# Attention and a mixture of experts: one scale per batch in place of a scale per token for the attention output, the second batch's values read twice, every step issued in a new order

## The chip, the cores and the metric

One Trainium2 chip, one of its cores. The time is device microseconds of one execution of the whole kernel; the number that counts is the median of three runs. The engines work side by side, each through its own queue in order: PE (TensorE, matmuls, with PEld for the loading of its stationary operand), DVE (VectorE), ACT (ScalarE), POOL (GpSimd) and SP (here only the issue of DMAs).

## The reference

Two parts, one behind the other: attention in which each query keeps only its 32 highest scores, and a dense mixture of four experts on its output.

```python
B, H, S, D = 2, 8, 576, 64
scores = (1 / np.sqrt(D)) * np.matmul(q, k.transpose(0, 1, 3, 2))
kth = np.partition(scores, -32, axis=-1)[..., -32:-31]
scores = np.where(scores >= kth, scores, -1e9)
attn = np.exp(scores - np.max(scores, axis=-1, keepdims=True))
attn = attn / (np.sum(attn, axis=-1, keepdims=True) + 1e-9)
x = np.matmul(attn, v).transpose(0, 2, 1, 3).reshape(B * S, H * D)   # 1152 x 512
p = domain_probs / (domain_probs.sum(-1, keepdims=True) + 1e-9)      # 1152 x 4
out = sum(p[:, e:e + 1] * (np.maximum(x @ w1[e], 0) @ w2[e]) for e in range(4))
```

## The kernel before

**Tiles and units.** The 1152 tokens are ten tiles: four of 128 rows and one of 64 in each batch. The 64-row tile of batch 0 comes first. A unit is one head of one tile (for a 64-row tile two heads side by side, 64 partitions each), so there are 72 units: 0 to 3 are the first tile, 4 to 11 the second, and so on; batch 1 begins at unit 36.

**A unit** goes through: scores on PE into PSUM (`emit_qk`, tile `ps`, two buffers); four MAX8 and three MATCH_REPLACE8 on DVE (`topk_op`), which find the 32 highest; an exponential on ACT (`emit_exp`); the mask (`emit_mask`), for units 0 to 19 one DVE instruction that reads `ps` (line 697, "DVE w"), later mostly on ACT and POOL; a split of the weights into two float16 halves (`emit_a`); a DMA transposition on SP's queue (`emit_at`, tile `at`); and the product with the values (`emit_av`). The mask is the last reader of `ps`, so the scores of unit u wait for the mask of unit u-2.

**Split operands.** All large matmuls run in float16 with each operand as a high and a low half: x = hi + lo. `split` makes these: mode "a" scales the raw values in place on ACT, copies to float16 on ACT and subtracts on POOL (a "lo"); mode "d" copies with the scale on ACT and makes the lo with one DVE instruction. The scale is a power of two from the mean square (`pow2`: two or three small DVE instructions). Weights (32 quarter matrices, tiles `w`), keys (`khl`, `kt`), values (`vt`), queries (`qhl`) and the attention output (`xhl`) are all split so. For keys and values of batch 0 there is one scale for all heads (`prep_first`), for batch 1 one for each head (`prep_kv`, squares on ACT, a matmul with ones, `pow2`); the inverse of the value scales stands in `sv`, and `emit_x_half` multiplies by it.

**Attention output.** `emit_x_half` divides by the sum of the weights; `emit_x_end` then squares x on ACT (`x_square`, line 805), in a 64-row tile adds the two halves' squares with matmuls against `pmat` (`x_cross`, line 809), takes one scale per token (`x_total`, `pow2`), scales in place and copies on ACT (`x_hi`, lines 820 and 822), makes the lo on POOL or DVE, puts inverse scale times probability into `pf` (`x_lo`, line 834) and issues the transposition to `xt`.

**Experts.** `moe` runs 8 half steps of `m1` (x against `w1`, lines 906 to 908), `h_hi`/`h_lo` (relu and split), `m2` (lines 949) for each tile; `evac` multiplies by the column of `pf`, adds up over the experts and writes the tile out.

**Order.** Nothing is scheduled at run time. Each step is an event with a place, and the table `ISSUE`, written into the kernel, has for each event and each of its pieces the position in the order of issue. `MASKS`, `NB`, `X_LO`, `EVAC`, `KV1`, `V0`, `K0`, `W_MODE` say per step which engine does it. Raw queries, keys and values of batch 1 pass through the pool `raw`, which has two buffers; a load into it waits until the reader of the buffer's former content is done.

Of the kernel before, what the change touches and what calls it, by code (L numbers as in the profile page):

```python
# [40 lines left out]
    kb_k=-64, kb_v=-5, kb_load=2, kb_sq=14, kb_tot=18, kb_scale=24, kb_fin=29,  # L41
)
MANUAL = ('PE', 'DVE', 'Activation', 'Pool', 'SP')
H_LO = ('ddpd', 'pppppppp', 'pppppddp', 'pdpppppd', 'pppppppp', 'pppppppp', 'pppppppp', 'pppppppp', 'pppppppp', 'pppp')

MASKS = 'ddddddddddddddddddddrrrrrrrrrdrrrrrrrrrddrdrdrrrrrrrrrrrrrrrrrrrrrrrrrrr'
NB = 'aaaaddddddddddddddadpdddddddpdapppapapdadppappppppaaapaapappaaaaapaappap'

X_LO = "dpdppppppp"
Q_LO = 'pppppppppp'  # L50

W_MODE = 'aaaaaaadaaaaaaaaaaaaaaaaaaadaaaa'
# [1162 lines left out]
```

## Time and profile before

| what | value |
|---|---|
| median of three runs | 567.65 us (565.24 to 568.88) |
| the profiled execution | 569.06 us, its span 567.3 us |
| mean granted TensorE clock | 0.951 |
| PE busy | 514.7 us, 91% of the span |
| DVE busy | 450.2 us, 79% |
| ACT busy | 384.2 us, 68% |
| POOL busy | 367.6 us, 65% |

The profiled execution has 1.8 us around its span and lies 1.4 us above the median. Busy shares are means over stages that differ: what the time turns on is which engine has no idle time in which stage, so the rows further down are cut by stage.

### The profile page before, as it was taken

The page shows a single profiled execution, that of the slowest core. Times are in us where ns is not written, and L with a number is a line of the kernel's source. Part 1 is how long each engine was busy: PE and PEld are TensorE (multiplying, and loading weights), DVE is VectorE, ACT ScalarE, POOL GpSimd, SP SyncE. Part 2 cuts the span into 40 slices and gives each one's busy share as a digit, 9 for nine tenths or more (in the row PEclk, how much of TensorE's full clock was granted, in tenths as well). Part 3 has the DMA queues.
Part 4 walks back from the last instruction along what each step waited for, and adds up shares of the span by engine and source line. Part 5 has one row for each costly group of instructions (what it writes and reads, how often), then busy time and mean ns, then how long its engine had stood idle before and what let it go on. Part 6 is the DMA issues. An engine that isn't in the chain of part 4 may idle for free.

```text
span 567.3 us, 16339 instructions
## 1 busy us (share of the span) xinstructions
PE 514.7 (91%) x6680; PEld 387.4 (68%) x6680; DVE 450.2 (79%) x1008; ACT 384.2 (68%) x668; POOL 367.6 (65%) x414
## 2 busy tenths in 40 slices
PE   4878667585999999999999999999999999999996
PEld 3556555373876668777876877777677777667864
DVE  2898999999899999999999998999988984700101
ACT  2678989989466696887876987767867746342311
POOL 0065988997665875887676878768865783451311
PEclk9988578876999999999999999999999999999999
DMA  9687878952263344555655644353443232231000
GB/s 222 205 223 184 260 239 182 239 91 51 60 93 64 62 97 90 82 86 107 131 103 127 95 96 83 64 101 62 57 78 72 43 64 41 41 41 44 12 2 29
DMA packets 140460, 57.05 MB, mean 101 GB/s; under 512 B 128864, under 2 KB 132064, under 8 KB 140384
## 3 DMA queue, kind: packets, MB, share of 16 engines
q1 hardware_dynamic: 136960, 53.12, 44.6%
q10 hardware_dynamic: 3424, 2.88, 1.7%
q8 instruction: 52, 0.85, 0.6%
q14 instruction: 24, 0.20, 0.1%
HBM read 24.14 MB, written 2.36 MB: 47 GB/s over the span
## 4 chain that ended last, share of the span: by engine, by line
PE 67%; DVE 17%; POOL 4%; DMA 4%; issue 3%; ACT 2%; SPq 1%; DVEq 0%; POOLq 0%; ACTq 0%
PE m L949 26%; PE m L906 10%; PE m L908 9%; PE m L907 9%; DVE m L646 6%; PE av L755 4%; PE ps L633 4%; DVE w L650 3%; DVE w L648 2%; DVE w L697 1%; DMA at<-a 1%; POOL h L931 1%; DMA xt<-xhl 1%; PE m L489 1%; DVE vt L426 1%
## 5 line engine op out<-in xcount | busy, mean ns | idle before, releaser
L949 PE MATMUL m<-w,h 128*128 128x512 f16 (+1 forms) x960 | 198.6, 384 | 0.9 <-POOL h L931 0.9
L908 PE MATMUL m<-xt,w 128*128 128x128 f16 (+1 forms) x1280 | 199.3, 215 | 0.0
L906 PE MATMUL m<-xt,w 128*128 128x128 f16 (+1 forms) x1120 | 179.0, 215 | 0.0
L907 PE MATMUL m<-xt,w 128*128 128x128 f16 (+1 forms) x1120 | 178.9, 215 | 0.0
L646 DVE MAX8 m<-w 128x8 f32<-128x576 f32 x216 | 161.5, 754 | 3.4
L949 PEld LDWEIGHTS <-h 128*128 128x128 f16 (+1 forms) x960 | 83.9, 102 | 90.9 <-issue 2.7
L931 POOL TENSOR_TENSOR h<-hf,h 128x512 f16<-128x512 f32 x65 | 75.3, 1158 | 85.9 <-ACT hf L924 79.3
L908 PEld LDWEIGHTS <-w 128*128 128x128 f16 x1280 | 123.8, 99 | 0.0
L906 PEld LDWEIGHTS <-w 128*128 128x128 f16 x1120 | 108.9, 99 | 3.1 <-issue 0.6
L907 PEld LDWEIGHTS <-w 128*128 128x128 f16 x1120 | 108.5, 99 | 2.4
L650 DVE MATCH_REPLACE8 w<-m,w 128x576 f32<-128x576 f32 x144 | 106.8, 742 | 0.0
L717 POOL TENSOR_TENSOR a<-w,a 128x512 f16<-128x512 f32 x68 | 78.9, 1163 | 15.1 <-ACT a L715 13.3
L690 ACT ACTIVATE w<-ps,nb,es 128x576 f32<-128x576 f32 x68 | 56.3, 829 | 42.0 <-DVE m L646 29.8
L917 ACT ACTIVATE h<-m 128x512 f16<-128x512 f32 x72 | 42.5, 592 | 60.2 <-PE m L908 43.3
L646 DVE MAX8 m<-ps 128x8 f32<-128x576 f32 x72 | 54.4, 755 | 31.5 <-PE ps L629 11.0
L707 POOL TENSOR_TENSOR w<-w,d 128x576 f32<-128x576 f32 x47 | 60.0, 1279 | 23.4 <-ACT d L704 21.7
L715 ACT ACTIVATE a<-w 128x576 f16<-128x576 f32 x68 | 45.8, 678 | 12.6 <-POOL w L707 8.6
L633 PE MATMUL ps<-kt,qa 128*128 128x288 f16 x128 | 36.7, 304 | 19.1 <-DVE w L697 19.0
L648 DVE MATCH_REPLACE8 w<-m,ps 128x576 f32<-128x576 f32 x72 | 53.8, 747 | 0.0
L976 DVE SCALAR_TENSOR_TENSOR o<-m,pf,o 128x512 f32<-128x512 f32 (+1 forms) x15 | 11.2, 745 | 50.6 <-PE m L949 42.4
L924 ACT ACTIVATE hf<-m 128x512 f32<-128x512 f32 x65 | 38.5, 592 | 5.5 <-POOL h L931 5.3
L755 PEld LDWEIGHTS <-at 128*128 128x128 f16 (+1 forms) x1008 | 37.1, 101 | 6.9 <-DMA at<-a 2.6
(172 smaller groups left out, 826.0 us busy)
## 6 DMA issues: line engine op xcount, KB each, us to landing
w<-in_moe_w_dram SPq DMA_DIRECT2D x16, 1024.0 KB, 8.1
qraw<-in_q_dram SPq DMA_DIRECT2D x8, 256.0 KB, 3.7
qb<-qa SPq DMA_DIRECT2D x16, 128.0 KB, 2.6
out_dram<-o ACTq DMA_DIRECT2D x8, 256.0 KB, 2.1
at<-a SPq DMA_TRANSPOSE x68, 3.3
vraw<-in_v_dram SPq DMA_DIRECT2D x2, 512.0 KB, 7.3
kraw<-in_k_dram SPq DMA_DIRECT2D x4, 256.0 KB, 3.4
vraw<-in_v_dram SPq DMA_DIRECT2D x4, 256.0 KB, 3.3
```

Of the source, the lines that this page charges most:

```text
L633: PE.matmul(ps[:, 0:288], lhsT=src[:, x, :], rhs=kt[x].rearrange("p c n -> p (c n)")[:, ks], start=(j == 0), stop=(j == 1))
L646: DVE.max(m, s_t[u] if r == 0 else w_t[u])
L648: DVE.match_replace(rows2(w_t[u]), m, s_t[u], NEG)
L650: DVE.match_replace(w_t[u], m, w_t[u], NEG)
L707: POOL.tensor_tensor(w, w, g, op=OP.mult)
L717: POOL.tensor_tensor(a[:, 640:1152], w[:, 0:512], a[:, 0:512], op=OP.subtract)
L755: PE.matmul(o, lhsT=att[:, blk, ps], rhs=r, start=(i == 0), stop=(i == len(seq) - 1))
L906: PE.matmul(o, lhsT=HI[e, 0, c][:, fc], rhs=xs(0, c), start=(c == 0), stop=False)
L907: PE.matmul(o, lhsT=HI[e, 0, c][:, fc], rhs=xs(1, c), start=False, stop=False)
L908: PE.matmul(o, lhsT=LO[e, 0, c][:, fc], rhs=xs(0, c), start=False, stop=(c == 3))
L931: POOL.tensor_tensor(h[:, 1], hf, h[:, 0], op=OP.subtract)
L949: PE.matmul(y[z * 64:z * 64 + M, :], lhsT=h_t[es, qd][:, p // 2, h0:h0 + M], rhs=w, start=(fc == 0 and p == 0), stop=(fc == 7 and p == 2))
```

## The change

**Attention output.** `x_square`, `x_cross`, `x_total`, the scaling in `x_hi` and `pf` are gone, with `pmat`. The scale of x is now one number per batch, taken from the values: the inverse of the value scale times a constant goes into `ix`, the division in `emit_x_half` brings it in with the constant `K_X`, and `evac` takes `pn` (batch 0, multiplied once by `ix` in `norm_x0`) or `pniw` (batch 1, multiplied once in `v1_scale`).

**Values of batch 1.** They need one scale for all eight heads ahead of the first split. So they are loaded twice: first as `nraw` in four loads of two heads, each squared as a whole on ACT (`v1_square`), then one matmul with ones, a sum and `pow2`; later again as `vraw`, two heads at a time, for the split itself. `prep_kv` becomes `prep_k1` and does the keys alone.

**Modes and order.** `V0` and `K0` become "a" throughout, of the later units four instead of five are masked on DVE and other ones, `NB`, `EVAC`, `KV1`, `X_LO`, `H_LO`, `W_MODE` change in places, and `ISSUE` is a new table.

```diff
-MASKS = 'ddddddddddddddddddddrrrrrrrrrdrrrrrrrrrddrdrdrrrrrrrrrrrrrrrrrrrrrrrrrrr'
...
+MASKS = 'ddddddddddddddddddddrrrrrrrrrrrrrrdrrrrrrrddrdrrrrrrrrrrrrrrrrrrrrrrrrrr'
...
-V0 = 'daddaaaa'
-K0 = 'daadaaaa'
+V0 = 'aaaaaaaa'
+K0 = 'aaaaaaaa'
...
-C_QK, C_V0, C_X, C_W1, C_W2 = 11, 14, 5, 10, 14
+C_QK, C_V0, C_W1, C_W2 = 11, 14, 6, 14
+K_X = 2.0 ** 5
...
+        def v1_square(p):
+            r = raw1["n", p]
+            r = r.rearrange("p h c d -> p (h c d)")
+            ACT.activation(r.bitcast(BF16)[:, 0:10 * D], r, AF.Square, accum_out=v1[:, p:p + 1])
+
+        def v1_total():
+            vs1["pt"] = bank(ps_m2, "m2")
+            PE.matmul(vs1["pt"][:, 0:4], lhsT=ones, rhs=v1, start=True, stop=True)
...
             if t == tiles[0]:
-                DVE.tensor_scalar(r2, total, EPS, None, op0=OP.add)
+                DVE.tensor_scalar(r2, total, EPS, ix[:, 0:1], op0=OP.add, op1=OP.mult)
             else:
-                vs = sv_r if rest else sv[:, t[0], half * 4:half * 4 + 4]
-                DVE.scalar_tensor_tensor(r2, total, EPS, vs, op0=OP.add, op1=OP.mult)
+                DVE.tensor_scalar(r2, total, EPS, K_X, op0=OP.add, op1=OP.mult)
...
             def x_hi():
-                x = st["x"]
-                if X_LO[g] == "p":
-                    ACT.activation(x, x, AF.Copy, scale=st["s"])
-                    yield
-                ACT.activation(st["hl"][:, 0:n], x, AF.Copy, scale=1.0 if X_LO[g] == "p" else st["s"])
...
+                ACT.activation(hl[:, 0:n], x_t[t][:, 0:n], AF.Copy)
...
-            at(steps[0], x_square)
-            if rest:
-                at(steps[0] + 0.1, x_cross)
-            at(steps[1], x_total)
             at(steps[2], x_hi)
...
         for p in range(4):
...
+            at(f1 + P["kb_n"] + 8 * p, load_raw, "n", p)
+            at(f1 + P["kb_n"] + 8 * p + 7, v1_square, p)
```

What the new order does, at three places. In the names, `ps` with a number is one unit's scores, `vt` with a number one head's values of batch 0, `w` with a number one weight matrix.

On DVE, at the first pass over the scores of unit 8, before:

```order
L646 MAX m<-ps_904 128x8
L286 TENSOR_SCALAR wpt<-m_858 128x1
L697 SCALAR_TENSOR_TENSOR w<-ps_769,m,w 128x576
L648 MATCH_REPLACE w<-m,ps_904 128x576
L686 TENSOR_SCALAR nb<-m,es 128x1
L646 MAX m<-w 128x8
L426 SCALAR_TENSOR_TENSOR vt_143<-vraw_153,vps,vt_143 128x5x64
L650 MATCH_REPLACE w<-m,w 128x576
```

and now:

```order
L655 MAX m<-ps_883 128x8
L659 MATCH_REPLACE w<-m,w 128x576
L657 MATCH_REPLACE w<-m,ps_883 128x576
L655 MAX m<-w 128x8 x2
L1060 TENSOR_SCALAR pn<-pn,ix 128x20
L420 SCALAR_TENSOR_TENSOR w_124<-w_124,ws,w_125 128x1024
L281 TENSOR_SCALAR wpt<-m_843 128x1
L706 SCALAR_TENSOR_TENSOR w<-ps_815,m,w 128x576
```

The lo of a head's values has left this queue, `norm_x0` has come into it, and a weight lo has come into these rows (before, the one DVE weight lo of this part of the program stood eleven rows ahead of them).

On POOL, around the lo parts of the third weight matrix, before:

```order
L424 TENSOR_TENSOR vt_145<-vraw_153,vt_145 128x5x64
L424 TENSOR_TENSOR khl_152<-kraw_151,khl_152 128x5x64
L719 TENSOR_TENSOR a<-w,a 128x64
L424 TENSOR_TENSOR w_125<-w_125,w_126 128x1024
L834 TENSOR_SCALAR pf<-pn,xpr 128x4
L424 TENSOR_TENSOR w_125<-w_125,w_126 128x1024
L424 TENSOR_TENSOR w_125<-w_125 128x1024 x2
```

and now (the third matrix is called w_124 here):

```order
L418 TENSOR_TENSOR w_124<-w_124,w_125 128x1024
L726 TENSOR_TENSOR a<-w,a 128x512
L728 TENSOR_TENSOR a<-w,a 128x64
L418 TENSOR_TENSOR vt_139<-vraw_152,vt_139 128x5x64
L418 TENSOR_TENSOR vt_146<-vraw_152,vt_146 128x5x64
L418 TENSOR_TENSOR vt_143<-vraw_152,vt_143 128x5x64
L813 TENSOR_TENSOR xhl<-x,xhl 128x256
L418 TENSOR_TENSOR vt_142<-vraw_152,vt_142 128x5x64
L418 TENSOR_TENSOR w_124<-w_124 128x1024
```

Four of the eight value lo parts and the first tile's x lo now stand between two weight lo parts; `pf` is gone.

On SP, about a third of the way through its queue, now:

```order
L816 DMA_TRANSPOSE xt<-xhl 128x8x128
L325 DMA nraw<-in_v_dram 128x2x256
L328 DMA nraw<-in_v_dram 64x2x64 x2
L734 DMA_TRANSPOSE at<-a 128x9x128 x3
L325 DMA nraw<-in_v_dram 128x2x256
L328 DMA nraw<-in_v_dram 64x2x64 x2
L734 DMA_TRANSPOSE at<-a 128x9x128 x2
L325 DMA nraw<-in_v_dram 128x2x256
```

where before there were transpositions and query loads alone:

```order
L837 DMA_TRANSPOSE xt<-xhl 128x8x128
L725 DMA_TRANSPOSE at<-a 128x9x128 x2
L406 DMA qb<-qa 64x1024
L408 DMA qb<-qa 64x1024
L725 DMA_TRANSPOSE at<-a 128x9x128 x2
L400 DMA_TRANSPOSE qa<-qhl 128x8x128
```

The four `nraw` loads, three DMAs each, stand ahead of `at` transpositions that PE's value products wait for.

## Rows read from the trace of the kernel before

**Rows 1.** Stretches of the span: busy us of each engine (instructions), clock, DMA.

```profile
0.00:31.86 31.86, 21.05 (x166) 14.12 (x167) 18.97 (x50) 16.82 (x37) 2.13 (x16) 1.00 0.77 198
31.86:81.01 49.15, 35.32 (x449) 29.74 (x449) 46.73 (x108) 40.96 (x62) 38.63 (x32) 0.69 0.81 225
81.01:134.60 53.59, 33.45 (x565) 27.37 (x562) 51.48 (x129) 49.24 (x62) 49.62 (x39) 0.83 0.76 173
134.60:450.00 315.40, 312.49 (x3915) 235.61 (x3915) 296.38 (x649) 233.84 (x433) 232.45 (x282) 0.99 0.45 84
450.00:562.40 112.40, 112.35 (x1593) 80.55 (x1591) 35.16 (x75) 43.30 (x77) 44.73 (x49) 1.00 0.17 34
```

**Rows 2.** Waits of PE over the whole span: us in total, times, longest.

```profile
PE ps L633 <- DVE w L697: 19.0, 9, 4.8
...
PE av L755 <- DMA at<-a: 1.9, 2, 1.4
...
PE m L906 <- DMA xt<-xhl: 1.5, 2, 1.0
```

**Rows 3.** Timeline of PE: scores of unit 17; 48 first-layer matmuls, first and last.

```profile
134.63 0.40 PE L633 MATMUL ps<-kt,qa 128*128 128x288 f16 x1 [4.80 <-DVE w L697]
...
140.79 0.23 PE L906 MATMUL m<-xt,wx 128*128 128x128 f16 x1
...
143.43 0.22 PE L908 MATMUL m<-xt,w 128*128 128x128 f16 x1
```

**Rows 4.** DVE's groups in 0 to 134.6 us: busy us, mean ns of one.

```profile
L646 DVE MAX8 m<-w 128x8 f32<-128x576 f32 x49 | 36.2, 747 | 0.2
...
L426 DVE SCALAR_TENSOR_TENSOR vt<-vraw,vps,vt 128x320 f16<-128x320 f32 x3 | 4.4, 1474 | 0.0
L426 DVE SCALAR_TENSOR_TENSOR khl<-kraw,k0ps,khl 128x320 f16<-128x320 f32 x2 | 2.8, 1402 | 0.0
...
L686 DVE TENSOR_SCALAR nb<-m,es 128x1 f32<-128x1 f32 x13 | 2.5, 197 | 0.0
...
L1068 DVE TENSOR_SCALAR sv<-ones,vps 128x8 f32<-128x8 f32 x1 | 0.6, 622 | 0.0
...
L829 DVE SCALAR_TENSOR_TENSOR xhl<-x,xps,xhl 128x256 f16<-128x256 f32 x1 | 0.5, 460 | 0.0
```

**Rows 5.** Timeline of DVE: key lo parts, and small operations at 133 us.

```profile
25.94 0.53 DVE L426 SCALAR_TENSOR_TENSOR khl<-kraw,k0ps,khl 128x320 f16<-128x320 f32 x1
...
32.06 2.27 DVE L426 SCALAR_TENSOR_TENSOR khl<-kraw,k0ps,khl 128x320 f16<-128x320 f32 x1
...
133.65 0.20 DVE L686 TENSOR_SCALAR nb<-m,es 128x1 f32<-128x1 f32 x1
133.77 0.80 DVE L697 SCALAR_TENSOR_TENSOR w<-ps,m,w 128x576 f32<-128x576 f32 x1
```

**Rows 6.** Timeline of POOL at 31.9 us.

```profile
31.86 2.12 POOL L424 TENSOR_TENSOR w<-w,wx 128x1024 f16<-128x1024 f32 x1 [2.43 <-ACT wx L421]
```

**Rows 7.** ACT's groups in 0 to 134.6 us.

```profile
L418 ACT ACTIVATE vraw<-vraw,vps 128x320 f32<-128x320 f32 x5 | 2.6, 551 | 0.0
...
L820 ACT ACTIVATE x<-x,xps 128x512 f32<-128x512 f32 x1 | 0.7, 721 | 0.1
...
L805 ACT ACTIVATE xhl<-x 128x512 bf16<-128x512 f32 x1 | 0.6, 630 | 0.1
```

**Rows 8.** POOL's groups in 0 to 134.6 us.

```profile
L424 POOL TENSOR_TENSOR vt<-vraw,vt 128x320 f16<-128x320 f32 x5 | 4.2, 831 | 0.0
...
L834 POOL TENSOR_SCALAR pf<-pn,xpr 128x4 f32<-128x4 f32 x1 | 1.3, 1277 | 0.0
```

**Rows 9.** Groups of PE and DVE from 134.6 us to the end.

```profile
L449 PE MATMUL m<-kss,ones 128*128 128x2 f32 x16 | 2.6, 234 | 0.0
L976 DVE SCALAR_TENSOR_TENSOR o<-m,pf,o 64x512 f32<-64x512 f32 x3 | 2.2, 749 | 14.8 <-ACT o L971 8.1 <-PE m L949 6.7
```

**Rows 10.** Waits of SP's queue over the whole span.

```profile
SPq L725 <- PE av L755: 85.1, 24, 8.1
```

More of the change, by code (lines that the diff above doesn't have):

```diff
@@ L429, in flat, with prep_k1 @@
             return ap.rearrange("p c d -> p (c d)")
-        def prep_kv(kind, b, hs, raw, mode):
+        def prep_k1(hs, raw, mode):
             st = {}
@@ L438, in kv_square1 @@
                 for i, h in enumerate(hs):
-                    if kind == "k":
-                        jk, r = flat(kt[h]).bitcast(BF16)[:, 0:320], flat(raw(h))
-                    else:
-                        jk, r = vt[h][:, :, 0:D].bitcast(BF16), raw(h)
-                    ACT.activation(jk, r, AF.Square, accum_out=st["ss"][:, i:i + 1])
+                    ACT.activation(flat(kt[h]).bitcast(BF16)[:, 0:320], flat(raw(h)), AF.Square,
+                                   accum_out=st["ss"][:, i:i + 1])
                     if i < n - 1:
@@ L451, in kv_scale1 @@
             def kv_scale1():
-                ss, at_b = st["pt"][:, 0:n], (slice(None), b, slice(hs[0], hs[-1] + 1))
-                if kind == "k":
-                    yield from pow2(st, ss, C_QK, n, "k", inv=invk[at_b], inplace=True)
-                else:
-                    yield from pow2(st, ss, C_QK, n, "k", dst=sv[at_b], inplace=True, need_inv=False)
-            def finish(h):
-                sc = st["s"][:, hs.index(h):hs.index(h) + 1]
-                if kind == "k":
-                    hl = raw(h).bitcast(F16)
-                    tmp = kt[h].rearrange("p c n -> p (c n)")[:, 0:320].rearrange("p (c d) -> p c d", d=D)
-                    yield from split(lambda: tmp, hl[:, :, 0:D], raw(h), sc, mode[h])
-                    yield
-                    ACT.activation(hl[:, :, D:2 * D], tmp, AF.Copy)
-                    yield
-                    SP.dma_start_transpose(out=kt[h], in_=flat(hl))
-                else:
-                    yield from split(lambda: vt[h][:, :, 0:D], vt[h][:, :, D + 1:], raw(h), sc, mode[h])
@@ L471, in prep_kv @@
-            return kv_square1, kv_total1, kv_scale1, finish
-        def rest_inv(dst, src, b):
+                yield from pow2(st, st["pt"][:, 0:n], C_QK, n, "k", inv=invk[:, 1, hs[0]:hs[-1] + 1], inplace=True)
+            def finish(h):
+                hl = raw(h).bitcast(F16)
+                tmp = kt[h].rearrange("p c n -> p (c n)")[:, 0:320].rearrange("p (c d) -> p c d", d=D)
+                yield from split(lambda: tmp, hl[:, :, 0:D], raw(h), st["s"][:, hs.index(h):hs.index(h) + 1], mode[h])
+                yield
+                ACT.activation(hl[:, :, D:2 * D], tmp, AF.Copy)
+                yield
+                SP.dma_start_transpose(out=kt[h], in_=flat(hl))
@@ new lines, in prep_k1, with v1_scale @@
+            return kv_square1, kv_total1, kv_scale1, finish
+        vs1 = {}
+        def v1_square(p):
[5 more added lines that the diff above has]
+            PE.matmul(vs1["pt"][:, 0:4], lhsT=ones, rhs=v1, start=True, stop=True)
+        def v1_scale():
+            ss = stp.tile([128, 1], F32, tag="v1s", name="v1s")
+            DVE.tensor_reduce(ss, vs1["pt"][:, 0:4], axis=mybir.AxisListType.X, op=OP.add)
+            yield
+            yield from pow2(vs1, ss, C_V0, 1, "v1")
+            yield
+            DVE.tensor_scalar(ix[:, 1:2], vs1["inv"], K_X, None, op0=OP.mult)
+            yield
+            iwb = iwp.rearrange("p (g e) -> p g e", g=1).to_broadcast([128, 5, E])
+            DVE.scalar_tensor_tensor(pniw[:, 5:10], pn[:, 5:10], ix[:, 1:2], iwb, op0=OP.mult, op1=OP.mult)
@@ L474, in rest_inv, with v1_finish @@
+        def v1_finish(h):
+            raw = raw1["v", h // 2][:, h % 2]
+            yield from split(lambda: vt[h][:, :, 0:D], vt[h][:, :, D + 1:], raw, vs1["s"], KV1["v"][h])
+        def rest_inv():
             for z in range(2):
-                DVE.tensor_copy(dst[z * 64:(z + 1) * 64], src[z * 64:(z + 1) * 64, b, 4 * z:4 * z + 4])
+                DVE.tensor_copy(invk_r[z * 64:(z + 1) * 64], invk[z * 64:(z + 1) * 64, 1, 4 * z:4 * z + 4])
         HI, LO, wscale = {}, {}, {}
@@ L782, in emit_x_half @@
             DVE.tensor_tensor(x, av[:, :, 0:64], r.to_broadcast([128, 4, D]), op=OP.mult)
-        xT_t, pf_t = {}, {}
+        xT_t = {}
         xF = {}
@@ L796, in emit_x_end, with x_hi @@
         def emit_x_end(t, g, steps):
-            rest = t[2] == 64
-            n = 256 if rest else 512
+            n = 256 if t[2] == 64 else 512
             st = {}
-            def x_square():
-                st["x"] = x = x_t[t][:, 0:n]
+            def x_hi():
                 st["hl"] = hl = hlp.tile([128, 8, 2 * D], F16, tag="hl", name="xhl").rearrange("p h e -> p (h e)")
-                st["ss"] = ss = stp.tile([128, 1], F32, tag="xss", name="xss")
-                ACT.activation(hl.bitcast(BF16)[:, 0:n], x, AF.Square, accum_out=ss)
-            def x_cross():
-                for z in range(2):
-                    PE.matmul(cross_t[t][z * 64:z * 64 + 64], lhsT=pmat, rhs=st["ss"], start=True, stop=True)
-            def x_total():
-                ss = st["ss"]
-                if rest:
-                    ss = cross_t[t]
-                yield from pow2(st, ss, C_X, 1, "x")
-            def x_hi():
-                x = st["x"]
-                if X_LO[g] == "p":
-                    ACT.activation(x, x, AF.Copy, scale=st["s"])
-                    yield
-                ACT.activation(st["hl"][:, 0:n], x, AF.Copy, scale=1.0 if X_LO[g] == "p" else st["s"])
+                ACT.activation(hl[:, 0:n], x_t[t][:, 0:n], AF.Copy)
             def x_lo():
                 hl = st["hl"]
-                if X_LO[g] == "p":
-                    POOL.tensor_tensor(hl[:, n:2 * n], st["x"], hl[:, 0:n], op=OP.subtract)
-                else:
-                    DVE.scalar_tensor_tensor(hl[:, n:2 * n], st["x"], st["s"], hl[:, 0:n],
-                                             op0=OP.mult, op1=OP.subtract)
-                yield
-                pf_t[t] = pf = stp.tile([128, E], F32, tag="pf", name="pf", bufs=3)
-                pw = pn if g < 2 else pniw
-                POOL.tensor_scalar(pf, pw[:, group(t), :], st["inv"], None, op0=OP.mult)
+                eng = POOL if X_LO[g] == "p" else DVE
+                eng.tensor_tensor(hl[:, n:2 * n], x_t[t][:, 0:n], hl[:, 0:n], op=OP.subtract)
                 yield
@@ L838, in x_lo @@
                 xT_t[t] = xT
-            at(steps[0], x_square)
-            if rest:
-                at(steps[0] + 0.1, x_cross)
-            at(steps[1], x_total)
             at(steps[2], x_hi)
@@ L1025, in attn_moe_kernel @@
             POOL.memset(vt[h][:, :, 64:65], 1.0)
-        def make_pmat():
-            for z in range(2):
-                POOL.tensor_copy(pmat[z * 64:z * 64 + 64], ident[z * 64:z * 64 + 64, z * 64:z * 64 + 64])
         def norm_probs():
@@ L1067, in kv_total @@
                 yield
-                DVE.tensor_scalar(inv_all[:, 0, :], ones[:, 0:H], st["s" if kind == "v" else "inv"], None, op0=OP.mult)
+                if kind == "v":
+                    DVE.tensor_scalar(ix[:, 0:1], st["inv"], K_X, None, op0=OP.mult)
+                else:
+                    DVE.tensor_scalar(inv_all[:, 0, :], ones[:, 0:H], st["inv"], None, op0=OP.mult)
             def kv_finish(h):
@@ L1085, in attn_moe_kernel, with norm_x0 @@
                    [max(P["k0_fin"] + P["k0_pace"] * h, 10 * (h % 4) + P["kf"] + 0.1) for h in range(H)])
-        prep_first("v", vraw0.rearrange("p h c d -> p (h c d)"), sv, [P["v_gram"], P["v_diag"], P["v_tot"]],
+        prep_first("v", vraw0.rearrange("p h c d -> p (h c d)"), None, [P["v_gram"], P["v_diag"], P["v_tot"]],
                    [max(P["v_split"] + h * P["v_pace"], 10 * (h % 4) + P["av_first"] + 0.1) for h in range(H)])
-        at(P["pmat"], make_pmat)
+        def norm_x0():
+            DVE.tensor_scalar(pn[:, 0:5], pn[:, 0:5], ix[:, 0:1], None, op0=OP.mult)
         at(P["probs"], norm_probs)
         at(P["probs2"], norm_probs2)
+        at(P["probs2"] + 1, norm_x0)
         def swap_scratch():
```

60 lines of the change are left out of this document (30 added, 30 removed), and 326 rows, old and new, of the table ISSUE.

## The prediction, made before the changed kernel ran

> **What bounds the kernel now.** I read the stretches first. From 134.6 us on PE is never idle: 312.49 of 315.40 us and then 112.35 of 112.40 [rows 1], at a clock of 0.99 to 1.00, the upper of its two levels. There the time is PE's work, and what other engines do costs nothing as long as it stays ahead. Up to 134.6 us PE works 21.05, 35.32 and 33.45 us of three stretches; it is idle for 44.8 us and partly at the lower clock (0.69, 0.83). So 567.3 us is PE's work, plus 44.8 us of idle time at the front, 3 us in the long stretch, 4.9 us behind the last matmul.
>
> Then the waits of PE: 19.0 us of the front's idle time are one thing, scores that wait for a mask on DVE because the mask frees their PSUM buffer [rows 2]. The last such wait, 4.80 us, ends at 134.63 with the scores of unit 17 [rows 3]. DVE is the engine behind it: 46.73 of 49.15 and 51.48 of 53.59 us [rows 1]. But it is not alone: in the third stretch ACT (49.24) and POOL (49.62) are almost as full, while between 31.86 and 81.01 us ACT still has 8.2 and POOL 10.5 us free. So three things count: what leaves DVE's queue ahead of the mask that frees unit 17's scores, whether ACT and POOL can follow, and how much PE work has been done by then.
>
> **The change part by part.**
>
> *DVE's queue ahead of the sixteenth mask (unit 15).* The two orders, counted up to that mask, differ by these. Out: two key lo parts at 1.40 us, three value lo parts at 1.47, the first x lo 0.46, the filling of `sv` 0.62 [rows 4]; nine `nb` (to ACT and POOL), at 0.12 each by the distance of two starts [rows 5]; four small one-column operations net, at the same 0.12. That is 2.80 + 4.42 + 0.46 + 0.62 + 1.08 + 0.48 = 9.9 us. In: one MAX8 more 0.75, one 64-row accumulation of the output 0.75 [rows 9], the multiplication of `pn` 0.12 (a small operation, as above) to 0.62 (the like filling of `sv`), I take 0.62 [rows 4]. In all 2.1; net 7.8 us less. The lower bound comes from the five lo parts: one of them took 0.53 us and another, the same form, 2.27, while POOL was in a weight lo from 31.86 to 33.98 [rows 5, 6]. At 0.53 each the net would be 3.2 us. I take the means, since the waits really stood in this queue.
>
> The Trainium skill (SBUF — State Buffer, section "Who interferes with whom") says that a DVE operation with two SBUF inputs, or in a two-port mode, and a GpSimd operation that reads SBUF lock each other out for a whole instruction. By that rule `norm_x0`, a plain scaling in SBUF among POOL's weight lo parts, could wait for all of one of them (2.12 us), and the sum would lose some 1.5 us more; the two rows above agree with the rule for the lo parts, and no row shows `norm_x0`.
>
> *Where the five lo parts go.* Each costs ACT one scaling in place, 0.55 us, and POOL a lo of 0.83 [rows 7, 8]. ACT between 31.86 and 81.01 us: five scalings, +2.8, against the first x's square, 512 columns of which took 0.63 [rows 7] (half as many here), and the copies that need no scale any more: net about +1.9, so 42.9 us of work in a stretch of 49.15. POOL: the order puts four key lo parts ahead of its first weight lo, where it waited 2.43 us anyway [rows 6]; from there to the fourth weight matrix it gets three value lo parts, one split of weights, two `nb` and the x lo more, two key lo parts and `pf` (1.28 [rows 8]) less, net +1.8 on 38.6. So by work alone DVE would let this stretch shrink by about 7.5 us (4.42 + 2.27 + 0.46 + small ones), POOL by 8.7, ACT by 6.3. ACT is the tightest. It can't lose all of its idle time in a chain that alternates between engines; I take three quarters, 4.6 us.
>
> *Rest of the front.* Ahead of 31.86: one key lo, 0.5 us. Behind 81.01 the removals (`nb`, `sv`) and the additions (accumulation, MAX8) about cancel, and POOL's work is 1.1 us less: 0.2 us. **Front: 0.5 + 4.6 + 0.2 = 5.3 us.**
>
> *Order on PE.* At the scores of unit 17 the new order has issued 432 instead of 384 first-layer matmuls, at those of unit 21 the same 624, with 120 of the second layer in both. So nothing is owed later: what the front is shorter by, the end is earlier by. The new order of everything else costs nothing under this cover: PE has work queued, and DVE's 296.38 of 315.40 us leave it 19 us [rows 1]; without that cover each wait would count in full.
>
> *PE's work after the front.* Eight totals of ones against squares (each two passes, 16 rows, 2.6 us in all [rows 9]) become four and one: 3 x 0.33 = 1.0 us. The last tile's `x_cross` goes, some 0.4 us by the same row's price of four passes, part of it overlapped. **1.4 us, on the path.**
>
> *Waits after the front.* PE waited 1.5 us for `xt` in two places [rows 2]. The chain to `xt` loses a square (0.63), three small DVE operations and a scaling (0.72) [rows 7], over 1.5 us; the new order may spend this by putting the copies later, so I count half: **0.7 us.** The rest of ACT's and POOL's relief there (square, scaling, `pf` for eight tiles) is off the path: nothing.
>
> *The second load of the values.* Four loads of a third of a megabyte, between 134.6 and 450 us, where the DMA engines are 0.45 busy [rows 1]: no cost by themselves. Their cost could only come through SP's queue, below. ACT's four squares, `v1_total` on PE (counted above) and the small DVE operations behind it have over 100 us until the first value split: nothing.
>
> Sum: 5.3 + 1.4 + 0.7 = **7.4 us**. The profiled execution (569.06, span 567.3) would become 561.7; it lies 1.4 us above the median of 567.65, so the median becomes **560.3 us**.
>
> **The rivals.**
>
> *DVE was the whole bound.* The front shrinks by all of DVE's 7.8 us, since ACT's idle time was only its waiting for DVE (DVE's small rows are what it waited for). With 2.1 us from later, 9.9 in all: 557.8. If unit 17's scores moreover come that early with the 48 first-layer matmuls ahead of them that before stood behind (2.7 us, 56 ns each [rows 3]), PE has less left: 555.1. Against: ACT and POOL are over 90% busy in the third stretch.
>
> *ACT and POOL hold the front.* ACT's waits are for its own order and don't shrink; DVE then only idles more. The front gives 1 us (what stands ahead of the first weight lo and a little more), PE's work 1.4: 565.2. For it: in the third stretch POOL is 93% busy with weight lo parts, whose work stays.
>
> *SP's queue holds transpositions back, slower.* The second to fourth `nraw` load can wait for one of the two `raw` buffers, and all `at` behind it wait too, then the value products, and PE is in order. SP already stood 85.1 us in 24 waits for the product two units earlier, 3.5 us each, 8.1 the longest [rows 10], and PE felt only 1.9 us of it [rows 2], so there is slack. If three loads held the queue for 3.5 us with no slack left, PE would lose 10.6 us: 560.3 + 10.6 = 570.9, slower than before. It decides against the change from 2.5 us for each load.
>
> *The change doesn't do what it says*: the per-token scale was all hidden, the moved lo parts cost elsewhere what they save, and 567.6 stays.
>
> **How the numbers follow.** Forecast, 558.5 to 563: 45%. DVE the whole bound, 555 to 558.5: 17%. ACT and POOL hold, 563 to 567: 25%. SP's queue: 10%. Nothing: 3%. One per cent, 5.7 us, is about what a measurement of this kernel can tell from no change; faster by more than that is below 562.0. Of the forecast's cases some four in five lie there, with the second case and a tail of the third: 54%. SP's case is slower by over 1% only from 4.4 us for each load, with the unforeseen: 7%. Within 1%: 39%. Range: 555.0 (the second case's bound) to 568, which leaves out most of SP's case and the tails.
>
> **What the profile afterwards would show.** Right: the wait for unit 17's scores ends at about 129 us instead of 134.6; no `khl` or `vt` lo of batch 0 on DVE; DVE's stretch from the first weight lo to the fourth matrix about 4 to 5 us shorter and ACT's idle time in it down to some 2 us; PE's idle time from there on at or under 3 us; `nraw` loads with no wait of PE for `at` behind them. Wrong: the same or more PE idle time in the front with ACT or POOL as what DVE waits for (second rival); PE waits for `at` of several us between 150 and 260 us (third); or PE's work itself dearer by the new order, for instance by more changes between first and second layer, which I hold at nothing.

## The result and the profile after

The changed kernel takes **551.19 us** (median of four runs, 550.94 to 554.0) beside 567.4 for the kernel before (565.24 to 568.88): ratio **0.973**, 95% interval 0.968 to 0.977, faster by 2.3 to 3.2 per cent. The forecast was 560.3 us, the range 555.0 to 568.0: the sign was right, the size less than half of it. The profiled execution has a span of 549.5 us (567.3 before) and a mean granted clock of 0.961 (0.951).

Stretches of the kernel after, cut where [rows 1] were cut (first weight lo on POOL, fourth weight matrix, mask of unit 15, and from 440 us on): us, then busy us and instructions of PE, PEld, DVE, ACT, POOL, then clock, DMA share, GB/s.

```profile
0.00:30.18 30.18, 20.35 (x173) 14.51 (x173) 17.44 (x49) 17.82 (x39) 5.24 (x20) 0.87 0.96 258
30.18:74.36 44.18, 32.73 (x410) 26.93 (x411) 42.55 (x108) 41.88 (x64) 40.23 (x36) 0.78 0.88 252
74.36:123.77 49.41, 35.22 (x633) 27.76 (x630) 49.10 (x114) 47.09 (x64) 47.48 (x37) 0.87 0.73 168
123.77:440.00 316.23, 314.92 (x3944) 237.12 (x3942) 294.67 (x630) 226.60 (x412) 228.91 (x275) 1.00 0.43 87
440.00:544.60 104.60, 104.56 (x1517) 75.30 (x1515) 32.85 (x64) 38.92 (x67) 43.12 (x46) 1.00 0.14 33
```

Against [rows 1] the first three stretches became 1.7, 5.0 and 4.2 us shorter: 10.8 us up to the mask of unit 15 (by the unrounded rows), of which the prediction had 5.3. ACT's idle time in the second stretch went from 8.2 to 2.3 us. In the third, DVE is left with 0.3 us of idle time and POOL with 1.9.

From there on the program was measured at two more marks, the scores of unit 21 and the last matmul. Three stretches of the kernel before (mask of unit 15, scores of unit 21, last matmul), same columns:

```profile
0.00:134.57 134.57, 89.83 (x1174) 71.24 (x1175) 117.15 (x285) 107.00 (x159) 90.35 (x85) 0.82 0.78 198
134.57:164.55 29.98, 29.92 (x370) 22.23 (x370) 27.12 (x65) 19.29 (x31) 23.07 (x24) 0.91 0.32 63
164.55:562.40 397.85, 394.92 (x5137) 293.93 (x5135) 304.45 (x660) 257.88 (x479) 254.14 (x307) 1.00 0.38 71
```

The same three stretches of the kernel after:

```profile
0.00:123.77 123.77, 88.31 (x1210) 69.20 (x1211) 109.08 (x269) 106.78 (x165) 92.94 (x90) 0.84 0.84 220
123.77:149.53 25.76, 25.76 (x334) 19.35 (x331) 25.41 (x61) 18.50 (x32) 20.02 (x20) 0.98 0.32 66
149.53:544.60 395.07, 393.71 (x5127) 293.08 (x5125) 302.11 (x633) 247.03 (x448) 252.01 (x301) 1.00 0.36 74
```

So the 17.8 us by which the last matmul comes earlier in these two profiles (the medians differ by 16.2) are 10.8 up to the mask of unit 15, 4.2 between it and the scores of unit 21, and 2.8 behind. In the first, DVE's work fell by 8.1 us and its idle time by 2.7 (17.4 to 14.7); ACT's work stayed (107.0 and 106.8) and its idle time fell by 10.6 (27.6 to 17.0); POOL's work rose by 2.6 and its idle time fell by 13.4. In the second, PE issues 36 matmuls fewer and its clock is 0.98 instead of 0.91.

PE's waits in the kernel after, beside [rows 2] (us in total, times, longest):

```profile
PE ps L642 <- DVE w L706: 18.2, 8, 4.9
...
PE m L881 <- DMA xt<-xhl: 2.3, 1, 2.3
...
PE av L764 <- DMA at<-a: 1.2, 2, 0.9
```

The wait for a mask is hardly shorter in sum; it lies earlier now, and the scores of unit 17 have none. PE's timeline of the kernel after shows what stands there instead, beside [rows 3]: a first-layer matmul of the second tile that waits for its `xt`, the scores of unit 17, two blocks of 24 second-layer matmuls, and the scores of unit 21.

```profile
120.41 0.22 PE L881 MATMUL m<-xt,wx 128*128 128x128 f16 x1 [2.31 <-DMA xt<-xhl]
...
124.64 0.35 PE L642 MATMUL ps<-kt,qa 128*128 128x288 f16 x1
...
127.97 2.78 PE L924 MATMUL m<-w,h 128*64 128x512 f16 x24
...
131.72 2.78 PE L924 MATMUL m<-w,h 128*64 128x512 f16 x24
...
149.53 0.29 PE L642 MATMUL ps<-kt,qa 128*128 128x288 f16 x1
```

In the kernel before, PE's timeline shows the same block first at the lower and then at the higher clock:

```profile
136.44 4.42 PE L949 MATMUL m<-w,h 128*64 128x512 f16 x24
...
143.57 2.78 PE L949 MATMUL m<-w,h 128*64 128x512 f16 x24
```

The first of them stands 1.8 us behind the 4.80 us wait of [rows 3], and its 24 matmuls cost 1.64 us more than as many seven microseconds later. In the kernel after, the scores of unit 17 wait for nothing, and both blocks of 24 behind them take 2.78 us. The lower clock has not vanished: it now lies ahead of those scores, on the 48 first-layer matmuls, which stand where PE waited before. Stretches of the kernel after, from the first of the 48 to the scores of unit 17 and behind them (the granted clock stands behind POOL):

```profile
120.40:124.60 4.20, 4.19 (x48) 4.20 (x49) 4.17 (x5) 2.25 (x4) 1.89 (x2) 0.61 0.41 95
124.60:128.00 3.40, 3.40 (x57) 3.18 (x54) 3.29 (x7) 3.40 (x5) 3.40 (x4) 0.97 0.02 5
```

What let PE fill the time is the transposition of the second tile's x. On SP's queue it stood here before:

```profile
134.03 1.23 SPq L837 DMA_TRANSPOSE xt<-xhl  x1
```

and stands here after, 18.7 us earlier, while the front as a whole moved by 10.8:

```profile
115.30 1.24 SPq L816 DMA_TRANSPOSE xt<-xhl  x1
```

### The profile page after: what moved, and what is told of

It reads as the page before. It is cut to its first block, busy times and chain, and to the rows that moved or that the text cites. A ratio compares the mean times of both kernels' runs of the same rounds, so it can differ in the third digit from the quotient of the medians.

```text
span 549.5 us, 16260 instructions
## 1 busy us (share of the span) xinstructions
PE 507.8 (92%) x6666; PEld 381.6 (69%) x6666; DVE 438.1 (80%) x961; ACT 372.3 (68%) x643; POOL 365.0 (66%) x410
## 5 line engine op out<-in xcount | busy, mean ns | idle before, releaser
L659 DVE MATCH_REPLACE8 w<-m,w 128x576 f32<-128x576 f32 x144 | 106.8, 742 | 0.0
L716 POOL TENSOR_TENSOR w<-w,d 128x576 f32<-128x576 f32 x48 | 61.4, 1281 | 36.0 <-ACT d L713 27.9
L948 DVE SCALAR_TENSOR_TENSOR o<-m,pniw,o 128x512 f32<-128x512 f32 (+1 forms) x17 | 12.7, 746 | 65.9 <-PE m L924 51.7
```

What stands on the lines that cost most here:

```text
L659: DVE.match_replace(w_t[u], m, w_t[u], NEG)
L716: POOL.tensor_tensor(w, w, g, op=OP.mult)
```

## The experiments

Medians are device us. Where a difference to the kernel after is given in us, it is the difference of the two ratios to the kernel before, times 567.4, since the kernels ran on several chips. The interval of the kernel after (0.968 to 0.977) alone is 2.5 us on either side. Stretches are of one profiled execution each. Idle time "up to the mask" is the length of the stretch up to the mask of unit 15 less the engine's busy time in it. Line numbers are each kernel's own.

**The kernel before with all lo parts of batch 0 on POOL.**

```diff
-V0 = 'daddaaaa'
-K0 = 'daadaaaa'
+V0 = 'aaaaaaaa'
+K0 = 'aaaaaaaa'
```

> The kernel before, its order unchanged, with the five lo parts of batch 0's keys and values moved from DVE to ACT and POOL (V0 and K0 all a). If DVE's queue alone sets the front (theory DVE), the 7.2 us that these five took there go: 567.4 - 7.2 = 560. If ACT and POOL cap it, as the prediction had it: about 564 to 565. If the new order made the gain (theory order): 567 or slower, since the old order was not made for this.

Measured: 568.6, ratio 1.000 (0.997 to 1.003). Nothing is gained, as "theory order" had it. The stretch up to the mask of unit 15:

```profile
0.00:136.44 136.44, 91.79 (x1174) 72.81 (x1175) 111.13 (x280) 108.11 (x164) 93.02 (x90) 0.83 0.80 195
```

DVE has 6.0 us less to do and idles 7.9 us more (25.3). The old order has POOL do the five parts at places made for DVE. DVE's waits up to 48 us (the longest three; the last is the scale of the values), there:

```profile
DVE m L646 <- PE ps L589: 11.6, 3, 9.7
DVE m L495 <- PE m L489: 4.2, 2, 2.5
DVE vpt L286 <- PE m L1063: 2.1, 1, 2.1
```

and before:

```profile
DVE m L646 <- PE ps L589: 10.4, 2, 9.2
...
DVE m L495 <- PE m L489: 0.8, 1, 0.8
```

So most of what left DVE came back as waits for PE, up to 48 us. What held PE there is not shown: its own waits up to 48 us are nearly the same in both kernels.

**The kernel before with nearly all of the new work, in the old order.** The modes of the lo parts as above, `NB` of the first twenty units as after, and the chain of the attention output left out (x is not scaled per token; batch 1's values keep one scale per head). The other modes that changed with the new table (`W_MODE`, `X_LO`, `H_LO`, `EVAC`, `MASKS`, `KV1`) stay old.

```diff
+V0 = 'aaaaaaaa'
+K0 = 'aaaaaaaa'
...
-                ACT.activation(hl.bitcast(BF16)[:, 0:n], x, AF.Square, accum_out=ss)
...
-                yield from pow2(st, ss, C_X, 1, "x")
+                yield 1
+                yield 1
...
-                    ACT.activation(x, x, AF.Copy, scale=st["s"])
...
-                POOL.tensor_scalar(pf, pw[:, group(t), :], st["inv"], None, op0=OP.mult)
+                pf_t[t] = (pn if g < 2 else pniw)[:, group(t), :]
```

> The kernel before, its order unchanged, doing nearly the work of the changed one: lo parts as in b_lo_on_pool, NB of the first 20 units as after, and x neither squared nor scaled (no x_square, x_cross, x_total, no scaling in place, no pf, so x keeps its own size and the output lacks no factor). Batch 1's values keep their scale per head. Theory DVE: 567.4 - 9.9 for DVE's queue - 2 for what lies behind = 555 to 556. Theory order: 565 to 567.

Measured: 563.8, ratio 0.995 (0.992 to 0.998), 2.8 us faster: far from "theory DVE" (555 to 556), near "theory order" (565 to 567). The same three stretches as above:

```profile
0.00:131.10 131.10, 90.75 (x1170) 72.51 (x1171) 110.35 (x266) 106.90 (x164) 94.08 (x93) 0.81 0.82 203
131.10:161.14 30.04, 29.98 (x370) 22.25 (x370) 27.05 (x65) 19.34 (x30) 23.02 (x23) 0.91 0.32 63
161.14:557.20 396.06, 394.61 (x5133) 293.70 (x5131) 301.85 (x635) 247.85 (x456) 251.92 (x299) 1.00 0.40 72
```

By the profile the work alone is worth 3.5 us in the front, nothing between unit 15 and unit 21, and 1.8 behind. The kernel after has the same work on DVE, ACT and POOL within 1.3 us up to that mask, yet is 7.3 us sooner there: DVE's idle time is 20.8 here and 14.7 there, ACT's 24.2 and 17.0, POOL's 37.0 and 30.8. That is the share of the order, with the modes that changed with it.

Cut where [rows 1] were cut, the second and third stretch of this kernel are:

```profile
31.89:80.33 48.44, 35.18 (x457) 30.39 (x457) 43.08 (x110) 41.72 (x64) 40.23 (x36) 0.72 0.92 240
80.33:131.10 50.77, 34.50 (x554) 27.98 (x551) 48.77 (x109) 47.64 (x63) 50.18 (x41) 0.78 0.79 171
```

From the first weight lo to the fourth matrix the new work alone gains 0.7 us (49.15 to 48.44), ahead of it nothing, and 2.8 behind it.

**The kernel after with the five lo parts back on DVE.**

```diff
-V0 = 'aaaaaaaa'
-K0 = 'aaaaaaaa'
+V0 = 'daddaaaa'
+K0 = 'daadaaaa'
```

> The changed kernel with V0 and K0 as before: five lo parts back on DVE, order unchanged. Theory DVE at the price they had (1.4 to 1.5 us each): 551.2 + 7.2 = 558.4; at the price of one that met no POOL operation (0.53 each): 554. Theory order: 551 to 552.

Measured: 557.8, ratio 0.983 (0.980 to 0.986), 5.9 us slower than the kernel after. The stretch up to the mask of unit 15:

```profile
0.00:127.89 127.89, 87.04 (x1218) 68.87 (x1219) 113.02 (x274) 105.56 (x160) 89.84 (x85) 0.88 0.80 213
```

It is 4.1 us longer, DVE's work 3.9 us more, and its idle time nearly the same (14.9). Here "theory DVE" came near and "theory order" missed: the move that gains nothing in the old order is worth its whole price in the new one. Only 1.4 of the 4.1 us lie between the first weight lo and the fourth matrix (30.01 to 75.60), where the five lo parts but one key lo stand; the rest shows behind.

**The kernel after with old work in the new order.** The five lo parts on DVE, the old `NB` of twenty units, and for each tile the chain of the attention output spread over the time between its two steps (scaling by one, so the values stay; `x_cross` stays out).

```diff
+            for share, fn in ((0.05, sq), (0.35, tot1), (0.5, tot2), (0.65, tot3), (0.95, scale), (1.0, pf)):
+                add(share, fn)
```

> The changed kernel in its new order with the old work put back: five lo parts on DVE, NB of the first 20 units as before, and for each tile the square of x on ACT, three small DVE operations, a scaling in place on ACT that waits for them (by 1.0), and pf on POOL; x_cross stays out. Theory DVE: 551.2 + 7.2 + 1.1 + 1 to 2 = 561 to 562. Theory order: 552 to 554.

Measured: 574.7, ratio 1.011 (1.007 to 1.015): slower than the kernel before, where the two theories had 552 to 562. The mask of unit 15 ends at 132.29, 2.3 us sooner than before, with 3.1 us less work on DVE and ACT's the same; the loss lies behind unit 21, where PE idles 12.6 us. **The kernel after with the chain alone**, everything else as it is there:

> The kernel after (551.2) with the chain of the attention output put back for each tile (a square on ACT, three one-column DVE operations, a scaling by one in place on ACT, one small POOL operation), spread over the time that the new order has between the two steps around it; the lo parts of batch 0 and the small operations stay as in the kernel after. The run with all old work in the new order took 574.7, of which 6.6 are the lo parts. Theory E (the chain to the transposed x is what holds PE there, since the new order issues the steps behind it without room for it): most of the other 17 us, 562 to 568, as idle time of PE behind unit 21. Theory F (the one-column operations that went back to DVE make it): less than 4 us here, 551 to 555. My prediction counted 0.7 us for this chain behind the front.

Measured: 570.0, ratio 1.003 (1.000 to 1.007), 17.4 us slower than the kernel after: "theory E", with PE idle behind unit 21, and more than its 562 to 568. Its three stretches:

```profile
0.00:123.75 123.75, 87.72 (x1217) 69.19 (x1218) 109.10 (x275) 108.65 (x171) 93.04 (x92) 0.88 0.83 218
123.75:149.92 26.17, 25.48 (x328) 18.64 (x325) 25.39 (x59) 18.76 (x32) 21.34 (x21) 1.00 0.45 76
149.92:561.40 411.48, 399.34 (x5127) 296.36 (x5125) 305.21 (x658) 256.90 (x472) 254.58 (x309) 0.99 0.38 71
```

The front does not feel the chain (ACT's 1.9 us more go into its idle time), but behind unit 21 PE idles 12.1 us, in many waits, none of whose kinds has more than some 5 us, and is busy 5.6 us longer with as many matmuls. This is a price of putting the chain where nobody made room, by places of mine; taken out of the old order, the chain and all else gave 1.8 us there. So it shows that this order has no room for the chain at these places, not that the chain was worth 17 us.

**Fillers: which engine holds the new front?** Three kernels, each the kernel after with about 8 us of repeated work on one engine (a filler):

```diff
+                if o == 6 and 8 <= u < 19:
+                    DVE.max(m, w_t[u])
...
+            for _ in range(more_act):
+                ACT.activation(hi, raw, AF.Copy, scale=1.0)
...
+            if 8 <= u < 15:
+                POOL.tensor_tensor(a[:, 640:1152], w[:, 0:512], a[:, 0:512], op=OP.subtract)
```

> The kernel after (551.2) with 11 MAX8 repeated on DVE, one in each of units 8 to 18, 0.75 us each: 8.2 us more on DVE ahead of the mask of unit 15, nothing else changed. Theory A, DVE, ACT and POOL together are the bound between 75 and 120 us (each had 44 to 45 of 45 us there): 6 to 8 us of it show, 557 to 559.5. Theory B, DVE alone is the bound: 559.4 too, and the other two fillers cost at most 2 us. Theory C, my prediction's, ACT is the tightest: at most 4 us show here, 555 or less. In A and B the mask of unit 15 moves by about 8 us, and after unit 21 nothing is lost or won.

> The kernel after (551.2) with the copy to float16 of eight weight quarters (the 13th to the 20th) done twice on ACT: 8 x 1.05 = 8.4 us more on ACT between about 75 and 105 us, each also 1.05 us ahead of the lo on POOL. Theory A (DVE, ACT and POOL together are the bound): 5 to 8 us show, 556 to 559.5. Theory B (DVE alone): at most 2 us, 553. Theory C (ACT the tightest): all 8.4, 559.6, and more than for the DVE filler.

> The kernel after (551.2) with the first 512 columns of the lo of the attention weights of units 8 to 14 done twice on POOL: 7 x 1.16 = 8.1 us more on POOL. Theory A (three engines together): 5 to 8 us show, 556 to 559. Theory B (DVE alone): at most 2 us, 553. Theory C (ACT the tightest): at most 3 us, 554.

Measured: DVE 557.6, ratio 0.982 (0.979 to 0.985), 5.2 us over the kernel after; ACT 559.4, 0.984 (0.980 to 0.988), 6.5 us; POOL 559.8, 0.985 (0.982 to 0.987), 6.9 us. All three cost most of what they add in time. The stretch from 75 to 120 us, in the kernel after:

```profile
75.00:120.00 45.00, 31.22 (x571) 23.73 (x567) 44.69 (x109) 44.78 (x61) 44.88 (x36) 0.89 0.74 166
```

with the DVE filler:

```profile
75.00:120.00 45.00, 29.50 (x478) 21.70 (x475) 44.76 (x107) 41.10 (x55) 39.95 (x32) 0.85 0.61 150
```

with the ACT filler:

```profile
75.00:120.00 45.00, 27.41 (x430) 20.51 (x430) 37.28 (x94) 44.78 (x59) 37.31 (x29) 0.81 0.59 138
```

and with the POOL filler:

```profile
75.00:120.00 45.00, 28.71 (x451) 21.40 (x448) 40.02 (x98) 40.47 (x55) 44.51 (x36) 0.85 0.69 150
```

Whichever engine is given more stays full and the other two starve: with the ACT filler DVE falls from 44.69 to 37.28 us and POOL from 44.88 to 37.31. So no one engine holds the front while the other two follow with room to spare.

The expectation that the mask of unit 15 moves by the whole filler failed, though. It moved by 4.2 us for the 5.0 us of DVE's filler that lie ahead of it (three of the 11 MAX8 stand behind), by 4.0 for 8.1 us on ACT, and by 3.1 for 5.2 on POOL. The rest of the cost lies behind that mask; for POOL, 4.1 us of it in its profile lie behind unit 21. The price in time is thus not the front's alone.

**The same fillers in the kernel before.**

> The kernel before (567.7) with the same 11 MAX8 as in the DVE filler of the kernel after, one in each of units 8 to 18: 8.2 us more on DVE. Theory A' (in the old order the front is as tight on all three engines as in the new one): 6 to 8 us show, as in the kernel after (6.4). Theory D (the old order leaves gaps between the engines, so it has room for more work): at most 4 us show, 571.7 or less.

> The kernel before (567.7) with the same eight copies on ACT done twice: 8.4 us more on ACT between about 80 and 112 us, where ACT had 4 to 5 us free. Theory A' (as tight as the new order): 8 us show, as in the kernel after (8.2). Theory D (gaps in the old order): at most 4 us, 571.7 or less.

> The kernel before (567.7) with the same seven lo parts on POOL done twice: 8.1 us more on POOL. Theory A' (as tight as the new order): 8 us show, as in the kernel after (8.6). Theory D (gaps in the old order): at most 4 us, 571.7 or less.

Measured: DVE 573.3, ratio 1.009 (1.006 to 1.011), 4.8 us; ACT 575.6, 1.013 (1.009 to 1.017), 7.3 us; POOL 573.2, 1.009 (1.005 to 1.012), 4.9 us. "Theory D", room for more work in the old order, falls by these times for ACT alone: the intervals for DVE and POOL, about 3 to 7 us, take in its limit of 4. The mask of unit 15 says more. It moved by 4.2, 7.4 and 4.4 us, for 5.4 us of DVE's filler ahead of it, 8.1 of ACT's and 5.5 of POOL's: per us of added work 0.8, 0.9 and 0.8, beside 0.8, 0.5 and 0.6 in the new order. So the old order had no more room than the new one. With these prices the first experiment is worked out: 6.0 us off DVE (-4.8), 1.1 more on ACT (+1.0), 2.7 more on POOL (+2.2), about -1.6 us at that mask; its profile shows +1.9 there, and its times 0 with an interval of 1.7 us on either side. The prices make the gain small; that it is nothing they do not show. The new work in the old order comes to -2.5 us in the front (6.8 off DVE, 3.7 more on POOL), where the profile shows -3.5.

**The kernel after without the second load of the values.** Batch 0's value scale serves batch 1; the `nraw` loads, their squares, `v1_total` and its sum are out.

```diff
-            ACT.activation(r.bitcast(BF16)[:, 0:10 * D], r, AF.Square, accum_out=v1[:, p:p + 1])
...
-            PE.matmul(vs1["pt"][:, 0:4], lhsT=ones, rhs=v1, start=True, stop=True)
...
-            yield from pow2(vs1, ss, C_V0, 1, "v1")
...
-            at(f1 + P["kb_n"] + 8 * p, load_raw, "n", p)
+            at(f1 + P["kb_n"] + 8 * p, nothing)
```

> The kernel after (551.2) without the first load of the second batch's values: no nraw loads, no squares of them, no matmul with ones, sum and power of two; the scale of batch 0's values serves batch 1 as well, at the same places in the order. My prediction: the loads, ACT's four squares and the small operations cost nothing, PE's one matmul 0.3 us at most: 550.5 to 551.5, ratio to the kernel after 0.999 to 1.0. Rival, SP's queue: the loads hold transpositions back, and without them the time falls by 2 us or more, to 549 or less.

Measured: 551.0, ratio 0.971 (0.968 to 0.974), within the intervals the same as the kernel after. The second load costs nothing that these runs can tell.

**The kernel after with 48 first-layer matmuls one place later.** One entry of `ISSUE`, that of `m1` for the first half step of the second tile, now stands right behind the scores of unit 17 instead of ahead of them; no other engine's queue changes.

```diff
+ISSUE[1191] = (569.5,)
```

> The kernel after (551.2) with one entry of the order changed: the 48 first-layer matmuls of the second tile that stand ahead of the scores of unit 17 stand right behind them, where the old order has them; all other entries stay, and no other engine's queue changes. Theory G (work that PE does in the front's idle time is taken from the end, so the new order's 48 matmuls ahead of unit 17 are a gain of their own): the scores of unit 17 at 123.8 instead of 124.6, those of unit 21 some 1.8 us later (48 x 56 ns = 2.7, less the 0.9 by which unit 17's scores come earlier) and the time 553.0; up to 2 us more if PE, idle ahead of unit 17, comes back at the lower clock. My prediction's step (nothing is owed later: the matmuls in front count only by the scores of unit 21): 551.2, and the scores of unit 21 at 149.5 as before.

Measured: 557.2, ratio 0.978 (0.976 to 0.981), 3.1 us slower than the kernel after by the ratios, whose intervals just meet; the profile shows it more sharply. Its three stretches:

```profile
0.00:123.68 123.68, 84.92 (x1170) 65.84 (x1170) 109.16 (x269) 106.82 (x165) 92.92 (x90) 0.84 0.85 220
123.68:153.27 29.59, 29.54 (x370) 22.90 (x371) 25.35 (x59) 18.49 (x32) 20.07 (x20) 0.93 0.28 57
153.27:550.80 397.53, 393.81 (x5127) 293.14 (x5125) 302.73 (x633) 247.20 (x448) 252.58 (x301) 1.00 0.36 74
```

The front is the same to 0.1 us; the stretch from the mask to the scores of unit 21 is 3.8 us longer, with the 370 matmuls that the kernel before has there, 29.59 beside its 29.98 us. That is what "theory G" had (1.8 us, and up to 2 for the clock), and not the prediction's step. And PE's timeline shows the wait back in its old place:

```profile
123.73 0.42 PE L643 MATMUL ps<-kt,qa 128*128 128x288 f16 x1 [5.73 <-DVE w L707]
```

Of the 3.8 us, 36 matmuls at 56 ns are 2.0; the rest goes with the clock, 0.93 instead of 0.98. Another 2.5 us are lost behind unit 21 in this profile (PE idles 3.7 us there instead of 1.4).

## Why the prediction was wrong

**DVE's queue ahead of the sixteenth mask: right.** 7.8 us less were forecast, 8.1 measured (117.15 to 109.08). The five lo parts, 7.2 us of it [rows 4], are all gone from DVE.

**Where the five lo parts go: the right number by luck.** From the first weight lo to the fourth matrix 4.6 us were forecast (three quarters of 6.3 would be 4.7) and 5.0 measured (49.15 to 44.18), with ACT's work at 41.9 (42.9 forecast) and its idle time down by 5.9 of 8.2 us, just under three quarters. But it is not the moved work that gives them: with that work and nearly all of the rest in the old order, this stretch is 0.7 us shorter, and with the five lo parts back on DVE in the new order it is 1.4 us longer.

**The step that failed first is the sum of the front**, "0.5 + 4.6 + 0.2 = 5.3 us", which prices the work that each engine loses and has no term for the order. Measured are 1.7, 5.0 and 4.2. The new work in the old order gives 0.0, 0.7 and 2.8 of these, 3.5 in all; the order, with its modes, gives 1.7, 4.3 and 1.4, or 7.3 us on the same work. "Rest of the front" was wrong for the work too: removals and additions behind the fourth matrix do not cancel, since DVE has 2.7 us less to do there in the old order and 2.4 in the new. In the new order DVE has one MAX8 and one MATCH_REPLACE8 less in that stretch, and POOL one weight lo and one split of attention weights less; they stand elsewhere. What the prediction took as a cap (ACT and POOL nearly full, so they can't follow DVE) was read from the busy shares of one order. Counted from the same traces, up to the mask of unit 15, exactly one of DVE, ACT and POOL stands idle for 38.7 us in the kernel before, 35.1 with the new work in the old order and 21.1 in the kernel after, and all three work at once for 74.8, 76.8 and 85.4 us. All three are idle at once for 8.4, 8.5 and 6.8 us, hardly less. So the new order gains by having the three work side by side for longer.

**The second step that failed is "Order on PE"**: "nothing is owed later". It saw that 432 instead of 384 first-layer matmuls stand ahead of unit 17's scores, and priced them at 2.7 us in a rival, but held that only the equal counts at unit 21 matter. They matter where PE is idle ahead of one mark and busy behind it: matmuls moved across come out of the end. Measured are 4.2 us from the mask of unit 15 to the scores of unit 21, and moving the 48 back returns 3.8 of them. That is more than 2.7, because the lower clock that PE has behind a long wait (0.58 behind the 4.80 us) now falls on the 48 matmuls themselves, from 120.4 to 124.6 us, in time that was idle before; behind the scores of unit 17 it is 0.97. The move was possible since the transposition of the second tile's x comes at 115.3 us.

**Behind unit 21: right.** PE's work 1.2 us less (1.4 forecast), its idle time 1.6 us less (0.7 forecast), 2.8 together for 2.1. The two waits for `xt`, 1.5 us of which half was counted, are both gone. The new work in the old order gave 1.8, and the 1.0 between is PE's work, the totals that it kept (PE is busy for 394.61 us there and for 393.71 here): the order shows no gain there.

**The rivals.** "DVE was the whole bound" came nearest (557.8, or 555.1 with the 48 matmuls), yet its reason is not right: moving DVE's lo parts to ACT and POOL gives nothing in the old order, and more work on ACT or POOL costs as much as on DVE. "ACT and POOL hold the front" is half of the truth: they count as DVE does, but their idle time did shrink. "SP's queue holds transpositions back" did not happen: PE's wait for `at` is 1.2 us, and the run without the `nraw` loads is no faster. Of the lock that the Trainium skill describes (SBUF — State Buffer, "Who interferes with whom"), `norm_x0` met only the last 0.16 us of a weight lo on POOL, by chance of its place, so its row (below) says nothing for or against the 1.5 us.

**What stays open** is which entries of `ISSUE`, or which of the modes that changed with it, make the 7.3 us in the front. The two orders differ in too many entries to undo them one by one, and the 7.3 us rest on one profile of each kernel. That the same work goes faster in the new order does not hang on them: by the ratios the kernel after is 12.6 us faster than the new work in the old order, as by the two profiles.

## What to carry to other kernels

Where three engines alternate and each is over nine tenths busy, price a change by fillers on each of them, not by the one that looks fullest, and put the whole filler ahead of the mark where you read it. Work that moves from one engine to another gives the difference of two prices; here the same move was worth nothing in one order and its whole price in another, so a price holds for the order in which it was measured. Of a new order, count how much work of the engine that bounds the end stands ahead of the place where it idles; what moves there is a gain of its own, which a later mark with equal counts hides.

## What the runs showed of the hardware

**Behind three waits here PE came back at the lower clock, for several microseconds.** Stretches of the kernel before: 7.5 us in which PE is busy for 1.31 and which the 4.80 us wait of [rows 3] ends, the 6 us behind it, and what follows; the granted clock stands behind POOL:

```profile
127.10:134.60 7.50, 1.31 (x18) 0.85 (x19) 7.44 (x14) 6.57 (x11) 5.75 (x6) 0.66 0.31 62
134.60:140.80 6.20, 6.17 (x43) 3.14 (x42) 6.20 (x15) 6.18 (x10) 4.60 (x3) 0.58 0.23 44
140.80:146.30 5.50, 5.50 (x75) 3.96 (x74) 4.07 (x11) 2.98 (x5) 5.50 (x7) 1.00 0.02 5
```

With 48 matmuls moved back behind the scores of unit 17, and so a wait of 5.73 us ahead of them, the same comes back:

```profile
123.70:131.70 8.00, 7.97 (x100) 7.53 (x100) 7.96 (x17) 8.00 (x14) 7.53 (x5) 0.73 0.01 2
131.70:137.00 5.30, 5.30 (x58) 2.85 (x58) 1.51 (x5) 0.53 (x1) 4.34 (x7) 1.00 0.26 58
```

In the kernel after it is the 0.61 from 120.40 us on, shown with the result, behind a wait of 2.31 us for `xt`. The upper level is 1.00 (2.4 GHz); 0.58 and 0.61 are near the lower one (1.2 GHz). The new order, which puts work into the wait, so saves more than that work's own length: the slow stretch falls into what was the wait.

**A DVE subtraction and POOL's hold each other up, in both directions.** In the kernel after, DVE's timeline has `norm_x0` and then a weight lo:

```profile
67.19 0.21 DVE L1060 TENSOR_SCALAR pn<-pn,ix 128x20 f32<-128x20 f32 x1
67.32 2.22 DVE L420 SCALAR_TENSOR_TENSOR w<-w,ws,w 128x1024 f16<-128x1024 f32 x1
```

and POOL's timeline beside them:

```profile
65.21 2.14 POOL L418 TENSOR_TENSOR w<-w 128x1024 f16<-128x1024 f32 x1
67.30 1.16 POOL L726 TENSOR_TENSOR a<-w,a 128x512 f16<-128x512 f32 x1
68.41 1.30 POOL L728 TENSOR_TENSOR a<-w,a 128x64 f16<-128x64 f32 x1
```

The small lo of POOL took 1.30 us, where the same form at 60.68 us took 0.31: it ended 0.2 us behind the DVE instruction. That one in its turn began with POOL's of 1.16 us, whose end left it 1.08 us. The Trainium skill (SBUF — State Buffer, "Who interferes with whom") says that of such a pair (a DVE instruction with two SBUF inputs, a GpSimd instruction that reads SBUF) the one that issues first has the ports for its whole instruction, and the other waits; the two rows agree with it. Read so, half of the weight lo's 2.22 us on DVE is waiting, and it costs POOL about 1.0 us as well. The run with the five lo parts back on DVE agrees: there the same weight lo began at 69.76 us, 0.19 us ahead of POOL's lo of values, and took 1.27 us, and POOL's took 1.73 where another took 0.79 (at 60.94 us in the kernel after).
